# Chunk pairs: input halves added by accumulating DMAs, the second pair's parts kept in DRAM, out products held back for two phases

## The chip, the cores and the metric

One core of one Trainium2 chip runs the whole program. The metric is the device time of one execution in microseconds. Five engines work side by side, each through its own list of instructions in order, and they wait for one another through semaphores: TensorE (PE; its weight loads are shown apart as PEld), VectorE (DVE), ScalarE (ACT), GpSimd (POOL) and SyncE (SP, which here only issues DMAs). An instruction that waits holds up all that stand behind it on its engine.

## The reference

Attention with a learned position bias, then a gated feed-forward network on its result:

```python
scores = q @ k.T / sqrt(64) + bias        # 4 batches, 8 heads, 576 positions
x = (softmax(scores) @ v)                 # as 2304 tokens of 512
gate = 1 / (1 + exp(-(x @ w_gate)))       # 512 x 1536
out = (gate * (x @ w_val)) @ w_out        # 1536 x 512
```

All is float32. Only the feed-forward part, the last 475 us, is touched by the change.

## The kernel before, in words

The attention part writes its result to DRAM as two halves, `xs` (1024 rows by 2304 tokens, to be added in pairs of 64 rows), and the reciprocals of the softmax sums, `rs`. An input piece for the feed-forward part is made by loading both halves (`load_x`, L796), adding them, and multiplying by the reciprocals (`load_r`, L805). The tokens are cut into six chunks of 384. Each float32 factor of a product is split into a high part, written by ScalarE with rounding to the matmul's format, and a low part, the difference, written by VectorE; a product is three matmuls: high x high, high x low, low x high.

*The first pass* (`run`, the loop over `order`) takes chunks 0 (A) and 1 (B) through the 12 blocks of 128 hidden units, in the order that `ORDER` writes out: 24 steps. A step has the gate products (`gates`, L887, 24 matmuls of 384 columns into the banks `pg` and `pu`), the out products of the step before (`outs`, `out`, L908, 9 matmuls of 512 columns into `po0` to `po2`, which is three groups of three), and the gating (`gated`, L895 to L898: sigmoid, product with a VectorE instruction, high part, low part). Beside it `convert` turns weight blocks into their parts: integer steps on VectorE (L190, L193, L196, L199), the high part on ScalarE (L850) and the low part on VectorE (L855). 30 of the 36 blocks are converted in this way, two in an A step and one in a B step. The converted gate weights are stored to DRAM (`scratch`, L859) for later.

In the same pass the inputs of chunks 2 and 3 are prepared. `pair_x` is a generator, and `XPIECES` says how many of its pieces run after which step: eight pieces that load two 192 KB halves each, add them on GpSimd (L931), load the reciprocals and multiply on VectorE (L944); four sums or differences of the quarters on GpSimd (L950: S1 to S4); and seven splits (ScalarE L958, VectorE L959).

*The phases* (`phase`) then take two chunks and two blocks at a time by a seven-product scheme (Strassen's, in Winograd's form): seven products of sums of inputs with sums of weights in place of eight. `STEPS` lists them. There are 24 phases, v = 0 to 11 for chunks 2 and 3 and v = 12 to 23 for chunks 4 and 5; an even v makes the gate's products, an odd v the value's. A phase step has 6 matmuls of 384 columns (L1054) into `pu` and `pg` by turns and, in six of seven steps, one group of three out products from the list `groups`. VectorE makes the additions and the gating (L1020), ScalarE empties the first bank (L1060) and makes sigmoids and high parts (L1028, L1038), GpSimd makes the low parts of the gated values (L1040).

The weights of phase v come from `unit(v, ...)`: "l" loads the stored blocks from `scratch` (L975, tile `um`), "t" makes four sums on GpSimd (L983, tile `ut`), "a" to "d" split them (ScalarE L995, VectorE L998). What a phase does beside its products is the list `beside[i]` for step i: "l" for v+2 at step 6, "t" for v+1 at step 0, "a" to "d" at steps 1 to 4, stores at steps 1, 3 and 5.

The inputs of chunks 4 and 5 (the second pair) go through `pair_x` in phases 1 to 10 too, in the tiles `xeven` and `xodd`, which chunks 0 and 1 have left; but their splits need the buffers of the first pair's parts, which come free only in phase 11, so `XPARTS` puts them into phases 11 and 12.

`take` hands out 4 KB buffers (per partition) from the pools `wfirst`, `wa` and `wb`, `give` returns them. Temporaries `st` share a pool of five (`wm`) with the converted weights. `store` (L921, L922) copies a finished `po` bank by ScalarE into a tile `ob`, of a pool of two, and sends it out.

The instructions of one engine run in the order in which these loops issue them. SP issues all DMAs of this part; GpSimd issues none.

Of the kernel before, what the change touches and what calls it, by code (L numbers as in the profile page):

```python
# [10 lines left out]
F32 = mybir.dt.float32  # L11
# [5 lines left out]
ALU = mybir.AluOpType  # L17
# [118 lines left out]
def tile_kernel(ctx, tc, q, k, v, small, w_gate, w_val, w_out, steps, lpos, xtab, lx, out, phases="0AB"):  # L136
# [4 lines left out]
    scratch = dram.tile([3 * DFF // 128, 128, 4, 128], F32, name="scratch")  # L141

    moe = Moe(tc, w_gate, w_val, w_out, scratch, xs, rs, out)
# [551 lines left out]
class Moe:  # L695
# [4 lines left out]
    def __init__(self, tc, w_gate, w_val, w_out, scratch, xs, rs, out):  # L700
        self.tc, self.nc, self.xs, self.rs, self.out_ = tc, tc.nc, xs, rs, out
# [213 lines left out]
    def store(self, c, t):  # L915
        n = 3 * c + t
        if c >= self.NC - 2 and n % 2:
            ob = self.pools["xin"].tile([128, 2, self.T], F32, name="xin").rearrange("p s t -> p (s t)")[:, 0:DM]
        else:
            ob = self.pools["ob"].tile([128, DM], F32, name="ob")  # L920
        self.nc.scalar.activation(out=ob, in_=self.po[c][t], func=AF.Copy)  # L921
        self.nc.sync.dma_start(out=self.out_[128 * n:128 * n + 128, :], in_=ob)  # L922

    def pair_x(self, c0, room):

        nc, x, loads, rows, parts = self.nc, {}, [], [], {}
        todo = [(c, kc) for c in (c0, c0 + 1) for kc in range(4)]
        name = lambda c, kc: f"A{c - c0 + 1}{kc // 2 + 1}"

        def add(j):  # L930
            nc.gpsimd.tensor_tensor(out=loads[j][:, 0], in0=loads[j][:, 0], in1=loads[j][:, 1], op=ALU.add)  # L931

        for j in range(len(todo) + 2):
            if j < len(todo):
                loads.append(self.load_x(*todo[j]))
            if 0 < j <= len(todo):
                add(j - 1)
                rows.append(self.load_r(*todo[j - 1]))
            if j > 1:
                c, kc = todo[j - 2]  # L940
                n = name(c, kc)
                if n not in x:
                    x[n] = room(n)
                nc.vector.tensor_tensor(  # L944
                    out=x[n][:, kc % 2], in0=loads[j - 2][:, 0], in1=rows[j - 2], op=ALU.mult)
            yield
        for o, a, b, op in (("S1", "A21", "A22", ALU.add), ("S3", "A11", "A21", ALU.subtract),
                            ("S2", "S1", "A11", ALU.subtract), ("S4", "A12", "S2", ALU.subtract)):
            x[o] = room(o)
            nc.gpsimd.tensor_tensor(out=x[o], in0=x[a], in1=x[b], op=op)  # L950
            if o == "S3":
                self.spare(x["A21"])
            yield
        self.parts[c0] = parts
        for n in ("A11", "S2", "A12", "S1", "S3", "S4", "A22"):
            hi = self.take([128, 2, self.T], F32R, "xh", "wa", "wb")
            lo = self.take([128, 2, self.T], F32R, "xl", "wa", "wb")
            nc.scalar.activation(out=hi, in_=x[n], func=AF.Copy)  # L958
            nc.vector.tensor_tensor(out=lo, in0=x[n], in1=hi.bitcast(F32), op=ALU.subtract)  # L959
            self.spare(x[n])  # L960
            parts[n] = hi, lo
            yield
# [121 lines left out]
    def run(self):  # L1084
# [4 lines left out]
        with ExitStack() as ph, tc.manual_schedule():  # L1089
            self.open(ph, "left", wa=SLOTS["wa"], wb=SLOTS["wb"], wm=WM, ob=2, sg=4, gv=6)  # L1090
# [4 lines left out]
            before, groups, stores, lows = None, [], [], []  # L1095
            xs = self.pair_x(2, lambda n: self.take([128, 2, self.T], F32, "xp", "wa", "wb"))
            for i, cf in enumerate(order):
# [13 lines left out]
                stored = before and before[1] == NF - 1  # L1111
# [3 lines left out]
                if stored:  # L1115
                    stores += [(0, t) for t in range(3)]
                if stores:
                    self.store(*stores.pop(0))
# [11 lines left out]
            for _ in xs:  # L1130
                pass

            def group(c, f, t, gh, gl):
                def do():
                    self.out(c, f, t, gh, gl)
                    if f == NF - 1:
                        stores.append((c, t))
                return do
# [3 lines left out]
            late, xs = [], iter(())  # L1142
            for v in range(NV):
# [3 lines left out]
                if v == 1:  # L1147
                    tiles = [self.pools[p].tile([128, 4, self.T], F32, name=n) for p in ("xeven", "xodd") for n in ("xhi", "xlo")]
                    homes = dict(zip(("A11", "A12", "A21", "A22", "S1", "S2", "S3", "S4"), (
                        y[:, 2 * e:2 * e + 2] for y in tiles for e in range(2))))  # L1150
                    xs, pieces = self.pair_x(4, homes.get), 14
# [57 lines left out]
```

## Time and profile before

| | us |
|---|---|
| median of three runs | 849.97 |
| the three runs | 843.79, 849.97, 853.77 |
| the profiled execution | 848.56 |
| its span | 846.5 |
| granted TensorE clock over the span | 0.978 |

The busy shares over the span are TensorE 94%, VectorE 77%, ScalarE 58%, GpSimd 50%. The profile shows one execution. Its span begins with the first instruction; times in the trace are counted from there. The attention part lasts to about 361, the first pass from there to 540, the phases to 833.5, and then twelve groups of out products are left. In the profile L12 is line 12 of the kernel, and `a<-b,c` means that tile a is written from tiles b and c. The chain of waits is followed back from the last instruction, at each step to what released it.

### The profile page before, as it was taken

To read this page: it belongs to the slowest core of one execution; us is meant where nothing else is said; L and a number is where in the kernel's file an instruction comes from. 1 tells how busy PE (TensorE), PEld (TensorE's weight loads), DVE (VectorE), ACT (ScalarE), POOL (GpSimd) and SP (SyncE) were. 2 spreads that over 40 slices of the span, in tenths; PEclk is the share of its full clock that TensorE was granted. 3 is DMA by queue.
4 is the path that set the end of the run, shared out by engine and by line. 5 is a ranking of instruction groups with operands and counts; after the bars stand their busy time and mean duration, and the time that the engine had idled before them with its cause. 6 is when DMAs were issued, how large, how long until landed. Compare 5 with 4: busy or idle time off the path is not lost.

```text
span 846.5 us, 17373 instructions
## 1 busy us (share of the span) xinstructions
PE 791.8 (94%) x6356; PEld 730.9 (86%) x6356; DVE 655.0 (77%) x1299; ACT 488.4 (58%) x1032; POOL 423.6 (50%) x476
## 2 busy tenths in 40 slices
PE   7999989999999988889997898978999999999997
PEld 4888879999999988878996797977889988899996
DVE  6788889999989988967887986457776787566673
ACT  5888588998989978834432343433334354334332
POOL 1333579999999979600021401154674353445430
PEclk9999999999999999989999898989999999999999
DMA  5532336565664687486669302145111102122001
GB/s 188 165 117 97 86 87 171 137 179 143 168 174 132 181 201 208 144 273 228 189 188 246 123 26 86 51 137 162 63 50 51 51 26 94 55 75 75 26 1 74
DMA packets 60931, 104.27 MB, mean 123 GB/s; under 512 B 6704, under 2 KB 28336, under 8 KB 60848
## 3 DMA queue, kind: packets, MB, share of 16 engines
q1 hardware_dynamic: 58544, 99.70, 40.2%
q10 hardware_dynamic: 2304, 3.47, 1.2%
q8 instruction: 50, 0.82, 0.4%
q14 instruction: 33, 0.27, 0.1%
HBM read 72.67 MB, written 21.05 MB: 111 GB/s over the span
## 4 chain that ended last, share of the span: by engine, by line
PE 61%; DVE 18%; DMA 7%; ACT 6%; issue 4%; POOL 2%; SPq 1%; DVEq 0%; ACTq 0%; POOLq 0%
PE po L908 12%; PE sc L549 7%; PE pu L1054 7%; PE pg L1054 7%; PE acc L629 7%; PE pt L572 5%; PE pu L887 4%; PE pg L887 4%; PE bps L342 3%; DMA xin<-xs 2%; DVE st L1020 2%; PE y L318 2%; DVE sg L1020 2%; ACT ind L323 2%; DMA um<-scratch 2%
## 5 line engine op out<-in xcount | busy, mean ns | idle before, releaser
L908 PE MATMUL po<-w,gh 128*128 128x512 f32 x432 | 136.2, 396 | 0.0
L556 ACT ACTIVATE en<-en,mn 128x576 f32<-128x576 f32 x144 | 111.5, 775 | 30.4 <-DVE mn L553 29.2
L549 PE MATMUL sc<-k,QS 128*128 128x288 f32 x640 | 112.1, 301 | 3.1 <-POOL k L476 0.7
L553 DVE CUSTOM_DVE_ANT_0 en<-sc,bias 128x576 f32<-128x576 f32 x128 | 93.9, 753 | 7.5 <-PE sc L549 6.4
L983 POOL TENSOR_TENSOR ut<-um 128x256 f32<-128x256 f32 x48 | 40.7, 868 | 110.6 <-DMA um<-scratch 55.5
L549 PEld LDWEIGHTS sc<-k,QS 128*128 128x128 f32 x640 | 91.7, 188 | 5.0 <-POOL k L476 1.2
L572 PE MATMUL pt<-ident,en 128*128 128x128 f32 x576 | 86.9, 273 | 3.4 <-DVE aL L472 2.3
L908 PE MATMUL po<-w,gl 128*128 128x512 f32 x216 | 85.5, 396 | 0.6 <-DVE gl L1040 0.6
L629 PE MATMUL acc<-aH,vv 128*128 128x288 f32 x256 | 80.3, 331 | 5.2 <-DVE xe L632 5.1
L1040 POOL TENSOR_TENSOR gl<-sg,gh 128x384 fp32r<-128x384 f32 x44 | 49.2, 1118 | 70.4 <-ACT gh L1038 48.0
L908 PEld LDWEIGHTS po<-w,gh 128*128 128x128 f32 x432 | 80.0, 190 | 4.8
L1038 ACT ACTIVATE gh<-sg 128x384 fp32r<-128x384 f32 x48 | 25.2, 525 | 93.9 <-DVE sg L1020 93.8
L572 PEld LDWEIGHTS pt<-ident,en 128*128 128x128 f32 x576 | 68.9, 141 | 6.2 <-ACT en L556 2.9
L472 DVE TENSOR_TENSOR aL<-pt,aH 128x512 fp32r<-128x512 f32 (+1 forms) x112 | 66.7, 608 | 7.2 <-ACT aH L471 7.2
L629 PE MATMUL acc<-aL,vv 128*128 128x288 f32 x256 | 71.0, 295 | 0.0
L342 PE MATMUL bps<-cfs,ind 128*128 128x64 bf16 x1458 | 67.4, 193 | 3.2 <-DVE bias L358 2.2
L323 ACT ACTIVATE ind<-y 128x576 bf16<-128x576 f32 x100 | 62.4, 657 | 11.0 <-PE y L318 8.9
L931 POOL TENSOR_TENSOR xin<-xin 128x384 f32<-128x384 f32 x16 | 18.3, 1155 | 97.9 <-DMA xin<-xs 79.1
L342 PEld LDWEIGHTS <-ind 128*128 128x128 bf16 x1458 | 58.6, 98 | 9.9 <-DVE bias L358 4.1
L887 PE MATMUL pu<-xhi,w 128*128 128x384 f32 x192 | 58.0, 363 | 9.4 <-DVE sg L896 9.0
L476 POOL TENSOR_TENSOR aL<-ar,aH 128x512 fp32r<-128x512 f32 x48 | 62.8, 1308 | 4.0
L1028 ACT ACTIVATE sg<-sg 128x384 f32<-128x384 f32 x48 | 25.2, 525 | 65.8 <-DVE sg L1020 65.8
(171 smaller groups left out, 2245.9 us busy)
## 6 DMA issues: line engine op xcount, KB each, us to landing
um<-scratch SPq DMA_DIRECT2D x48, 256.0 KB, 2.7
kr<-in_k_dram SPq DMA_DIRECT2D x32, 288.0 KB
QS<-part SPq DMA_DIRECT2D x64, 144.0 KB, 2.8
xs<-xe SPq DMA_DIRECT2D x32, 288.0 KB, 3.6
xin<-xs SPq DMA_DIRECT2D x48, 192.0 KB, 3.3
vr<-in_v_dram SPq DMA_DIRECT2D x16, 320.0 KB, 3.8
scratch<-wm SPq DMA_DIRECT2D x20, 256.0 KB, 2.2
qr<-in_q_dram SPq DMA_DIRECT2D x16, 288.0 KB
```

The lines of the kernel that those rows point to most:

```text
L323: nc.scalar.activation(out=o, in_=y[:, :, 0:HF], func=AF.Sigmoid, scale=float(2.0 ** 64))
L342: nc.tensor.matmul(out=o, lhsT=st, rhs=cfs[:, part], start=(part == 0), stop=(part == 2))
L472: return lambda: nc.vector.tensor_tensor(out=lo, in0=ps, in1=hi.bitcast(F32), op=ALU.subtract)
L476: nc.gpsimd.tensor_tensor(out=lo, in0=src, in1=hi.bitcast(F32), op=ALU.subtract)
L549: nc.tensor.matmul(out=ps[:, e, 0:HF], lhsT=l, rhs=r[:, HF * e:HF * e + HF], start=(i == 0), stop=(i == len(mms) - 1))
L553: nc.vector.tensor_tensor_reduce(out=half(en), in0=ps[:, :, 0:HF], in1=half(nbias), scale=-0.125, scalar=3.0e38, op0=ALU.add, op1=ALU.min, ...
L556: nc.scalar.activation(out=en, in_=en, func=AF.Exp, bias=mn, scale=-1.0, accum_out=sm)
L572: nc.tensor.transpose(pt[:, J], en[:, 128 * J:128 * J + 128], ident)
L629: nc.tensor.matmul(out=acc[:, 0:HF], lhsT=l, rhs=r, start=(i == 0), stop=(i == len(mms) - 1))
L887: self.nc.tensor.matmul(out=(pg, pu)[z], lhsT=l, rhs=r, start=(kc == 0 and i == 0), stop=(kc == 3 and i == 2))
L908: self.nc.tensor.matmul(out=self.po[c][t], lhsT=l[:, tt], rhs=r, start=(f == 0 and i == 0), stop=(f == self.NF - 1 and i == 2))
L1054: nc.tensor.matmul(out=y, lhsT=l, rhs=r, start=(n == 0), stop=(n == 5))
```

## The change

- `pair_x` becomes a function that runs named steps, listed for the first pass in `XPIECES` and for the phases in `XSTEPS`. "L" loads the first halves (SP), "A" adds the second halves onto them by DMAs with `accum_op=ALU.add` that GpSimd issues, "r" loads reciprocals, "M" multiplies on VectorE. Each step of these moves 64 rows of 384 at a time (96 KB), and two pieces share an `xin` tile.
- The sums S1 to S4 are made by VectorE; S3 is written over A21.
- "P" splits as before (first pair). For the second pair "Q" splits in phases 8 to 10: the high part into one tile `high`, the low part in place, and both are written to DRAM (`xparts`). "R" loads them in phase 11 into the buffers that the first pair's parts leave.
- The out products of steps 20 to 22 of the first pass are not issued in the pass but appended to `groups` (`HELD`), as those of step 23 were before, so twelve groups go into phases 0 and 1, and the stores of chunk 0 with them.
- "l" of unit v+2 is issued at step 2 of a phase, not at step 6.
- The tiles `ob` come from the pool of five (`wm`); `wb` has 17 buffers, not 16. "l0" to "d" of the first unit stand one step later in `UPIECES`.

```diff
-SLOTS = {"wfirst": 6, "wa": 15, "wb": 16}
-XPIECES = {8: 2, 9: 1, 10: 2, 11: 1, 12: 2, 13: 1, 14: 2, 15: 1, 16: 2, 17: 1, 18: 2, 19: 1, 20: 2, 21: 2, 22: 2, 23: 9}
-XPARTS = {11: (1, 3, 4, 6), 12: (0, 2, 4)}
-UPIECES = {18: "l0", 19: "t0", 20: "l1", 21: "a0 b0", 22: "c0 d0"}
+SLOTS = {"wfirst": 6, "wa": 15, "wb": 17}
+HELD = 20
+XPIECES = {
+    6: "L0 L1", 8: "A0 A1 r0 r1", 9: "L2 L3", 10: "M0", 11: "M1 r2 r3 A2 A3", 12: "L4 L5", 13: "M2", 14: "M3 r4 r5 A4 A5",
+    15: "L6 L7", 16: "M4", 17: "M5 r6 r7 A6 A7", 18: "M6", 19: "M7", 20: "S1 S3", 21: "S2 S4", 22: "PA11 PS2 PA12",
+    23: "PS1 PS3 PS4 PA22"}
+UPIECES = {19: "l0", 20: "t0 l1", 21: "a0 b0", 22: "c0", 23: "d0"}
+XSTEPS = {
+    (0, 1): "L0 L1 r0 r1", (0, 3): "L2 L3", (1, 1): "A0 A1", (1, 4): "A2 A3", (2, 0): "M0", (2, 1): "M1 r2 r3", (2, 2): "L4 L5",
+    (2, 4): "M2", (2, 5): "M3 r4 r5", (3, 1): "A4 A5", (3, 2): "L6 L7", (4, 0): "M4", (4, 1): "M5 r6 r7", (4, 2): "A6 A7",
+    (4, 5): "M6", (4, 6): "M7", (6, 0): "S1", (6, 2): "S3", (6, 4): "S2", (7, 0): "S4", (8, 0): "QA22", (8, 2): "QA12",
+    (8, 4): "QS1", (9, 0): "QS3", (10, 0): "QS4", (10, 2): "QA11", (10, 4): "QS2", (11, 0): "RA11", (11, 1): "RS2",
+    (11, 2): "RA12", (11, 3): "RS1", (11, 4): "RS3", (11, 5): "RS4", (11, 6): "RA22"}
...
+    xparts = dram.tile([7, 2, 128, 2, 384], F32, name="xparts")
...
-            ob = self.pools["ob"].tile([128, DM], F32, name="ob")
+            ob = self.pools["wm"].tile([128, DM], F32, tag="wm", name="ob")
...
+            if k in "LA":
...
+                for e in range(2):
+                    row = 256 * kc + 128 * e + (64 if k == "A" else 0)
+                    src = self.xs[row:row + 64, T * c:T * c + T]
+                    if k == "L":
+                        nc.sync.dma_start(out=half(j)[64 * e:64 * e + 64], in_=src)
+                    else:
+                        nc.gpsimd.dma_start(out=half(j)[64 * e:64 * e + 64], in_=src, accum_op=ALU.add)
...
+                x[n] = x["A21"] if n == "S3" else room(n)
+                nc.vector.tensor_tensor(out=x[n], in0=x[a], in1=x[b], op=op)
...
+            elif k == "Q":
+                hi, i = room("high"), order.index(n)
+                nc.scalar.activation(out=hi.bitcast(F32R), in_=x[n], func=AF.Copy)
+                nc.vector.tensor_tensor(out=x[n].bitcast(F32R), in0=x[n], in1=hi, op=ALU.subtract)
+                for z, t in enumerate((hi, x[n])):
+                    nc.sync.dma_start(out=self.xparts[i, z], in_=t)
+            else:
+                parts[n] = [self.take([128, 2, T], F32R, "xr", "wa", "wb") for _ in range(2)]
+                for z, t in enumerate(parts[n]):
+                    nc.sync.dma_start(out=t.bitcast(F32), in_=self.xparts[order.index(n), z])
...
-                    self.outs(*before)
+                    if i <= HELD:
+                        self.outs(*before)
+                    else:
+                        groups += [group(before[0], before[1], t, *before[2:]) for t in range(3)]
...
-                for _ in range(XPIECES.get(i, 0)):
-                    next(xs, None)
+                xs(XPIECES.get(i, ""))
...
+                for i in range(7):
+                    if (v, i) in XSTEPS:
+                        beside[i].append(lambda w=XSTEPS[v, i]: xs(w))
                 if v + 2 < NV:
-                    beside[6].append(lambda v=v: self.unit(v + 2, "l"))
+                    beside[2].append(lambda v=v: self.unit(v + 2, "l"))
```

## Rows read from the trace of the kernel before

**Rows 1.** Stages: us, busy PE, PEld, DVE, ACT, POOL, clock, DMA share, GB/s.
```profile
372.00:424.20 52.20, 51.40 (x256) 48.18 (x257) 41.77 (x79) 22.48 (x43) 0.00 (x0) 0.94 0.71 234
424.20:517.50 93.30, 80.34 (x388) 73.94 (x387) 80.58 (x127) 33.72 (x63) 19.06 (x14) 0.91 0.49 141
540.40:563.60 23.20, 18.47 (x94) 16.98 (x94) 12.40 (x24) 9.45 (x19) 5.69 (x6) 0.91 0.41 126
563.60:675.40 111.80, 107.44 (x541) 96.51 (x540) 81.11 (x126) 40.24 (x82) 65.21 (x67) 0.99 0.25 74
675.40:703.80 28.40, 25.43 (x122) 22.75 (x122) 22.38 (x33) 14.28 (x27) 12.10 (x12) 0.94 0.13 44
```

**Rows 2.** Chain of waits, first pass: start us, us, what.
```profile
420.00 2.08 PE pg L887 x12
...
424.16 2.05 PE po L908 x9
...
477.48 2.23 DVE wm L196
...
516.64 3.02 PE pu L887 x12
...
540.38 1.04 PE pu L1054 x6
```

**Rows 3.** VectorE's groups, 393 to 424.2: instruction, shapes, count | busy us, mean ns | idle before.
```profile
L199 DVE SCALAR_TENSOR_TENSOR wm<-ww,wm 128x512 int32<-128x512 int32 x8 | 5.5, 692 | 0.3
L855 DVE TENSOR_TENSOR w<-wm,w 128x512 fp32r<-128x512 f32 x8 | 5.5, 685 | 0.0
L190 DVE TENSOR_SCALAR wm<-wm 128x512 f32<-128x512 f32 x9 | 3.8, 420 | 0.0
L193 DVE TENSOR_SCALAR wm<-wm 128x512 int32<-128x512 int32 x8 | 3.4, 420 | 0.0
```

**Rows 4.** VectorE's groups, 424.2 to 517.5.
```profile
L199 DVE SCALAR_TENSOR_TENSOR wm<-ww,wm 128x512 int32<-128x512 int32 x18 | 15.5, 860 | 0.6
L855 DVE TENSOR_TENSOR w<-wm,w 128x512 fp32r<-128x512 f32 x20 | 15.0, 752 | 0.0
L196 DVE SCALAR_TENSOR_TENSOR wm<-ww,wm 128x512 int32<-128x512 int32 x18 | 14.0, 776 | 0.6
L193 DVE TENSOR_SCALAR wm<-wm 128x512 int32<-128x512 int32 x18 | 10.0, 557 | 0.0
L190 DVE TENSOR_SCALAR wm<-wm 128x512 f32<-128x512 f32 x17 | 9.5, 561 | 0.0
L898 DVE TENSOR_TENSOR gl<-sg,gh 128x384 fp32r<-128x384 f32 x12 | 6.7, 559 | 7.1 <-ACT gh L897 7.1
...
L944 DVE TENSOR_TENSOR xp<-xin,xrec 128x384 f32<-128x384 f32 x8 | 5.3, 659 | 3.0 <-DMA xrec<-rs 3.0
L959 DVE TENSOR_TENSOR xl<-xp,xh 128x768 fp32r<-128x768 f32 x4 | 3.8, 953 | 1.0 <-ACT xh L958 1.0
```

**Rows 5.** GpSimd's groups, 424.2 to 517.5.
```profile
L931 POOL TENSOR_TENSOR xin<-xin 128x384 f32<-128x384 f32 x8 | 8.8, 1103 | 94.5 <-DMA xin<-xs 79.1 <-DVE wm L190 8.4 <-DVE wm L196 7.0
L950 POOL TENSOR_TENSOR xp<-xp 128x768 f32<-128x768 f32 x4 | 8.5, 2141 | 10.9 <-DVE xp L944 10.8
```

**Rows 6.** Chain of waits, phase 1.
```profile
551.79 4.50 DMA um<-scratch
```

**Rows 7.** Chain of waits, a phase at full pace.
```profile
763.02 1.04 PE pg L1054 x6
764.06 1.06 PE pu L1054 x6
765.11 0.70 PE po L908 x3
```

**Rows 8.** Line L796: issues on SP's queue, ns least/median/most, first and last start.
```profile
L796 SPq DMA_DIRECT2D xin<-xs x48: 573/605/946, 292.6 to 595.5; - x48
```

**Rows 9.** DMA issues by line: count, KB each, median us from issue to landing.
```profile
xin<-xs SPq DMA_DIRECT2D x48, 192.0 KB, 3.3
```

More of the change, by code (lines that the diff above doesn't have):

```diff
@@ L698, with __init__ @@
     NC = NT // T
[L700 to L701 removed]
+    def __init__(self, tc, w_gate, w_val, w_out, scratch, xparts, xs, rs, out):
+        self.tc, self.nc, self.xs, self.rs, self.out_, self.xparts = tc, tc.nc, xs, rs, out, xparts
         self.src = {}
@@ L927, in pair_x @@
[L927 to L941, printed above, removed]
+        nc, T = self.nc, self.T
@@ new lines, in pair_x, with do, half, one @@
+        x, loads, rows = {}, {}, {}
+        parts = self.parts[c0] = {}
+        order = [a for a, _ in self.STEPS]
+        def do(what):
+            for w in what.split():
+                one(w[0], w[1:])
+        def half(j):
+            return loads[j // 2][:, j % 2]
+        def one(k, n):
+            j = int(n) if k in "LArM" else 0
+            c, kc = c0 + j // 4, j % 4
+            if k in "LA":
+                if k == "L" and j % 2 == 0:
+                    loads[j // 2] = self.pools["xin"].tile([128, 2, T], F32, name="xin")
+                for e in range(2):
[5 more added lines that the diff above has]
+                        nc.gpsimd.dma_start(out=half(j)[64 * e:64 * e + 64], in_=src, accum_op=ALU.add)
+            elif k == "r":
+                rows[j] = self.load_r(c, kc)
+            elif k == "M":
+                n = f"A{c - c0 + 1}{kc // 2 + 1}"
@@ L942, in pair_x @@
                 if n not in x:
                     x[n] = room(n)
[L944 to L962, printed above, removed]
+                nc.vector.tensor_tensor(out=x[n][:, kc % 2], in0=half(j), in1=rows[j], op=ALU.mult)
+            elif k == "S":
+                n = k + n
+                a, b, op = self.SUMS[n]
+                x[n] = x["A21"] if n == "S3" else room(n)
+                nc.vector.tensor_tensor(out=x[n], in0=x[a], in1=x[b], op=op)
+            elif k == "P":
+                hi = self.take([128, 2, T], F32R, "xh", "wa", "wb")
+                lo = self.take([128, 2, T], F32R, "xl", "wa", "wb")
+                nc.scalar.activation(out=hi, in_=x[n], func=AF.Copy)
+                nc.vector.tensor_tensor(out=lo, in0=x[n], in1=hi.bitcast(F32), op=ALU.subtract)
+                self.spare(x[n])
+                parts[n] = hi, lo
+            elif k == "Q":
[8 more added lines that the diff above has]
+                    nc.sync.dma_start(out=t.bitcast(F32), in_=self.xparts[order.index(n), z])
@@ L1129, in run @@
                 g()
[L1130 to L1138, printed above, removed]
             groups += [group(before[0], before[1], t, *before[2:]) for t in range(3)]
             NV = 2 * NF
-            late, xs = [], iter(())
+            tiles = [self.pools[p].tile([128, 4, self.T], F32, name=n) for p in ("xeven", "xodd") for n in ("xhi", "xlo")]
+            homes = dict(zip(("A11", "A12", "A21", "A22", "S1", "S2", "S4", "high"), (
+                y[:, 2 * e:2 * e + 2] for y in tiles for e in range(2))))
+            late, xs = [], self.pair_x(4, homes.get)
             for v in range(NV):
```

31 lines of the change are left out of this document (11 added, 20 removed).

## The prediction

> **What bounds the kernel now.** I read the table of stages first. The reader is to see that TensorE is the nominal limit, busy for all but a few us of most stages, and that three stages are exceptions: 424.2 to 517.5 (80.3 us busy of 93.3, granted clock 0.91), 540.4 to 563.6 (18.5 of 23.2, clock 0.91) and 675.4 to 703.8 (25.4 of 28.4, clock 0.94) [rows 1]. Only there can time be won, unless matmuls go, and none do.
>
> Second, the chain in order of time through the first pass. At full pace a step is 2.08 us for each of the two gate products and 2.05 for the out products, 6.21 us in all. Step 8 begins at 420.00 and the first phase at 540.38: 120.4 us for 16 steps that need 99.4, so 21.0 are lost [rows 2]. The chain there goes through VectorE: VectorE paces this stretch, and TensorE waits for converted weights or for a bank to be emptied.
>
> Third, VectorE's groups, before the pair loads begin and while they run. A conversion is five instructions, 0.69 (L199, and L196, which is the same operation on the same shape), 0.69, 0.42 and 0.42 us at pace [rows 3]. In the loaded stretch the same five mean 0.86, 0.78, 0.75, 0.56 and 0.56 [rows 4]. In that stretch GpSimd makes eight adds of 1.10 us and four sums of 2.14 us [rows 5], and beside a sum VectorE's 0.69 us instruction takes 2.23 [rows 2]. So GpSimd's arithmetic costs VectorE its own time. Besides, VectorE stands 3.0 us in its multiply for reciprocals that have not landed, and 1.0 us for ScalarE in the splits [rows 4].
>
> **The change, first pass.** What VectorE is relieved of up to the end of the conversions, from [rows 3, 4]: (860-692)x18 = 3.0, (752-685)x20 = 1.3, (776-692)x18 = 1.5, (557-420)x18 = 2.5, (561-420)x17 = 2.4, together 10.7; the multiplies lose 0.8 more (659 against 559 for the other 384-wide instruction, x8). The waits of 3.0 and 1.0 go, since each half is now loaded two steps before its accumulate and the accumulate about two before the multiply, some 12 us each, where a load lands in 3.3 [rows 9]. Four split subtractions of 0.95 (3.8 us) move behind the conversions. Sum: 19.3 us.
>
> That assumes that an accumulating DMA does not hold VectorE back. The trace of before has no DMA issued by GpSimd. At worst each holds VectorE as the add did, the adds' share of 11.5 us: 11.5 x 8.8/17.3 = 5.9. At best nothing is held; a gain below nothing is not to be had, as the lock of the adds is counted already. I take nothing, since no elements of the input pass through GpSimd any more, and keep 5.9 for the range.
>
> The gate products of step 20 end at 519.66 now [rows 2]. Less 19.3 that is 500.4. TensorE alone would be there at 420.00 + 12x6.21 + 4.16 = 498.7, so VectorE is still last, by 1.7.
>
> From there to the first phase it is 20.7 us now. In the changed kernel TensorE has 2.05 (out products of step 19) and three steps of 4.16, 14.5, because nine held groups (9x0.70) leave. VectorE has more than before: the four sums, at 0.95 each by the 768-wide subtraction of [rows 4], and the splits. I walk it: gating (0.56, a wait of 7.1/12 = 0.59 for ScalarE, 0.56, [rows 4]) and two sums end at 504.0; the gate products of step 21 are there at 506.6; gating, two sums and a unit's low part (0.69, as the same 512-wide instruction of [rows 3]) end at 510.9; step 22 is there, gating, three splits (3x0.95+1.0) and a low part end at 517.2; the multiply of step 23 frees the bank at 517.7. So the first phase starts at **517.7** instead of 540.4. If VectorE hid behind TensorE it would be 514.9; if nothing is won in these steps, 521.1. The four remaining splits (3.8 us) then delay phase 0's own additions, and a phase step with its groups lasts 1.75: I put 1.5 us for it.
>
> **The phases.** At pace a step is 1.05 and a group 0.70 [rows 7]; 24 phases have 168 steps. Now 135 groups lie between the start and 833.5, so 270.9 of 293.1 us: 22.2 lost. In the changed kernel 144 groups lie there (the held twelve fill phases 0 and 1 with six each): 277.2 us, then the tail after 833.5, 13.0, unchanged. The losses by stage [rows 1], before and then after:
> - Phases 0 and 1: 23.2 less 14x1.05+3x0.70 is 6.4. The chain shows a weight load that is on its way only from 551.8, for 4.5 us, then GpSimd's differences [rows 6]. The load now stands at step 2 of a phase, not step 6, behind eight input loads of 0.6 [rows 8] and one store: about 7 us into phase 0, where it is at 11 now, and the phase is 2.1 longer. Next late are the four splits: 1.5.
> - Phases 2 to 10: 111.8 less 9x11.55 is 7.9. GpSimd's adds and sums go; four sums (3.8) and seven split subtractions (6.7) come to VectorE, which is busy 81 of 112 us there: room for them. Added waits: ScalarE may not write the single `high` tile again before its 384 KB write to DRAM has landed. A 192 KB load lands in 3.3 [rows 9], and writes follow by two steps, 3.5: between nothing and 1 us, three times. SP now waits for each split before it issues; behind it stand weight loads with some 8 us in hand. I take 3.5.
> - Phases 11 and 12: 28.4 less 23.1 is 5.3, the splits of the second pair. They become 14 loads, 5.5 MB. The DMA rate at full share is 141/0.49 to 234/0.71, 288 to 330 GB/s [rows 1]: 2.4 to 2.7 us for a pair of loads, one pair issued every 1.65, each due some 10 after. With one weight load between, the seventh lands about 23 after phase 11's start and is due at 21.5. At 330 it costs nothing, at the unscaled 234 some 7. I take 2.5, near the rate at full share.
> - Phases 13 to 23: the rest of the 22.2, 2.6; a weight load issued at step 6 can be late there too, and step 2 gives it 7 us more; 1.0.
>
> Sum: 517.7 + 277.2 + 1.5+3.5+2.5+1.0 + 13.0 = 816.4 us of span against 846.5. The profiled execution took 848.56, 2.06 over its span, and stands 1.4 below the median shown: 816.4+2.06+1.4 = **820**. The extra buffer slot and the out buffers taken from the shared pool cost nothing where they are hidden by TensorE; if a store held the pool, a temporary waits for a landing of some 2 us, in phases 0, 1, 12 and 13 only.
>
> **What GpSimd's queue does.** It loses 16 adds and 8 sums, 35 us at [rows 5]'s means, and gets 32 DMA issues. Bounds of one: nothing, or as long as a load takes to be issued and to land, 0.95+3.3 = 4.2 [rows 8, 9], if the engine were held; I take 1.0, nearest to SP's 0.6 and to the add it replaces. In phases 2 to 10 GpSimd is busy 65.2 us; less eight adds and four sums (17.4) that is 5.3 a phase. In phases 1 to 4 (46.2 us) it has 21.2 to do and 16 issues: full only at 1.6 us each. In the first pass it has nothing else.
>
> The Trainium skill speaks against this part ("DMA: Bandwidth & Descriptors", SWDGE vs HWDGE vs iDMA): for a DMA issued from GpSimd the descriptors are written by GpSimd into SBUF, state that VectorE shuts it out of in its two-port mode, and a DMA issued from SP is immune. By that rule the issues would be slowest where VectorE is fullest. No run here shows it yet; the rival below prices it.
>
> **Rivals.**
> 1. *Slower: GpSimd's queue paces phases 1 to 4.* The weight differences stand behind the accumulates in order. Decides from 1.6 us per issue; at 4.2 it is 16x4.2+21.2 = 88.4 in 46.2, 42 late: 862. For it: nothing like it was measured, VectorE is dense. Against: SP issues in 0.6.
> 2. *No change: the accumulated halves land late, or wait for the first half, so VectorE stands at the multiplies as it does now.* Eight multiplies that each wait the 3.0 us which [rows 4] has for all of them give back 24: 844. Against it: about 24 us of lead.
> 3. *Half the gain: VectorE stays locked by the accumulates (5.9) and the parts come late from DRAM (5 more than taken):* 831.
> 4. *Better: VectorE hides behind TensorE and the phase losses nearly vanish:* 514.9+277.2+2+13.0+3.5 = 811, or below.
>
> **How the numbers follow.** Forecast 820 (811 to 829): 0.60. Rival 3: 0.13. Rival 2: 0.10. Rival 1: 0.12. Below 811: 0.05. The range 809 to 845 leaves out rival 1 and the far ends of the others. One per cent, 8.5 us, is about what a measurement of this kernel can tell from no change. Faster by more: forecast, rival 3, the low end and nothing of rival 2: 0.77. Within: 0.11. Slower: 0.12.
>
> **What would show it.** Right: first phase near 518; VectorE's 0.42 us instructions at 0.42 between 424 and 500; no wait of VectorE for a load at the multiply; weight differences in phase 1 ready before the step that needs them; no split in phases 11 and 12, and TensorE waiting there at most 3 us, for loads. Wrong: GpSimd holding over 1.6 us per accumulate, or VectorE waiting at multiplies; TensorE waiting for parts from DRAM through phase 12; VectorE so full in steps 20 to 23 that the first phase starts after 521.

## The result and the profile after

The changed kernel takes 821.25 us (median of four runs, 819.7 to 825.87); the kernel before took 847.29 in the four runs that count beside it. A fifth run of the changed kernel, 817.06, is not in that median. The ratio is 0.9682, with a 95% interval from 0.961 to 0.9753: faster, by 26 us, where 820 was forecast in a range of 809 to 845.

The profiled execution is the slowest of these runs, 825.87 us with a span of 824.1. Its attention part is 2.1 us longer than before (step 8 of the first pass begins at 421.96, not at 419.83), which the change doesn't touch. So I compare stages by their length, each from its first matmul to that of the next, read from the timeline of TensorE:

| stage | before | forecast | after |
|---|---|---|---|
| first pass, step 8 to phase 0 | 120.4 | 97.7 | 101.1 |
| phases 0 and 1 (nine groups more after) | 23.4 | 24.6 | 27.8 |
| phases 2 to 10 | 111.8 | 107.5 | 109.3 |
| phases 11 and 12 | 28.4 | 25.6 | 23.2 |
| phases 13 to 23 | 129.7 | 128.1 | 127.4 |
| the rest | 13.0 | 13.0 | 13.3 |

The stages of the changed kernel, with the columns of [rows 1]; the first is the 93.4 us from step 8's out products on, the others are the stages of the table:

```profile
426.30:519.70 93.40, 89.67 (x477) 84.00 (x476) 76.10 (x136) 36.24 (x68) 13.76 (x16) 1.00 0.52 151
523.10:550.90 27.80, 25.13 (x121) 22.74 (x122) 19.30 (x30) 13.95 (x26) 15.21 (x18) 0.95 0.41 110
550.90:660.20 109.30, 105.72 (x542) 95.85 (x540) 89.10 (x137) 45.69 (x91) 61.20 (x65) 1.00 0.39 122
660.20:683.40 23.20, 23.20 (x121) 21.47 (x122) 17.00 (x27) 10.16 (x21) 10.71 (x13) 1.00 0.87 314
683.40:810.90 127.50, 127.50 (x662) 117.99 (x662) 87.94 (x142) 48.06 (x100) 53.70 (x59) 1.00 0.15 48
```

TensorE is busy for 89.7 of 93.4 us where it was for 80.3 of 93.3, and its granted clock there is 1.00 in place of 0.91. In phases 11 and 12 and from 13 on the profile shows no idle time of it.

The clock has a part of its own in this. In the kernel before, it was granted at 0.50, the lower of its two levels (1.2 GHz), in three stretches of together 17 us, from 463.9, 484.4 and 511.7 on, each time in or right after a wait of TensorE of 3.7 to 4.4 us; the last of them, in the columns of [rows 1]:

```profile
511.70:518.50 6.80, 5.43 (x17) 5.43 (x18) 5.49 (x8) 2.50 (x5) 2.67 (x3) 0.50 0.11 42
```

The gate product of 3.02 us in [rows 2], which takes 2.08 at pace, lies for the most part in it. In the changed kernel the clock does not fall from step 8 until the wait just ahead of phase 0.

VectorE's groups over the same 93.4 us answer to [rows 4] (all line numbers from here on are ten to forty higher than before):

```profile
L865 DVE TENSOR_TENSOR w<-wm,w 128x512 fp32r<-128x512 f32 x20 | 14.1, 711 | 0.0
L206 DVE SCALAR_TENSOR_TENSOR wm<-ww,wm 128x512 int32<-128x512 int32 x18 | 12.9, 715 | 0.6
L209 DVE SCALAR_TENSOR_TENSOR wm<-ww,wm 128x512 int32<-128x512 int32 x18 | 12.5, 692 | 0.6
...
L203 DVE TENSOR_SCALAR wm<-wm 128x512 int32<-128x512 int32 x18 | 8.3, 461 | 0.0
L200 DVE TENSOR_SCALAR wm<-wm 128x512 f32<-128x512 f32 x17 | 7.1, 419 | 0.0
L976 DVE TENSOR_TENSOR xp<-xin,xrec 128x384 f32<-128x384 f32 x8 | 4.4, 551 | 0.0
L981 DVE TENSOR_TENSOR xp<-xp 128x768 f32<-128x768 f32 x4 | 3.8, 955 | 0.1
```

A conversion is nearly back at its pace, and the multiplies (L976) wait for nothing. What took the place of GpSimd's adds: all 32 accumulating DMAs, the length of their records on GpSimd in ns (least, median, most), from the view of their line; one group of four of them from the timeline; and the stretches of this and of another group, in the columns of [rows 1]:

```profile
L969 POOL DMA_DIRECT2D xin<-xs x32: 803/1378/2185, 415.4 to 583.3; - x32
```
```profile
540.96 3.31 POOL L969 DMA_DIRECT2D xin<-xs  x4
```
```profile
540.96:544.27 3.31, 3.31 (x19) 3.08 (x18) 0.74 (x2) 0.65 (x2) 3.31 (x5) 1.00 0.82 216
546.84:550.19 3.35, 3.35 (x19) 3.08 (x19) 3.20 (x6) 1.31 (x3) 3.35 (x6) 1.00 0.52 112
```

The records of four issues in a row overlap, so their lengths do not add up: seven of the eight groups of four hold GpSimd for 3.3 to 3.5 us and the first, at 415.4, for 4.0. That is 0.8 to 1.0 us for each. The DMA issues with KB and median us to landing:

```profile
xr<-xparts SPq DMA_DIRECT2D x14, 384.0 KB, 4.8
xparts<-xlo SPq DMA_DIRECT2D x10, 384.0 KB, 2.3
...
xin<-xs POOLq DMA_DIRECT2D x32, 96.0 KB, 4.9
```

And the place that went worse than forecast, the splits on either side of the start of phase 0 (523.05); those shown stand before it, and the four behind it run in the same way. The timeline of VectorE, then that of ScalarE:

```profile
517.23 0.96 DVE L986 TENSOR_TENSOR xl<-xp,xh 128x768 fp32r<-128x768 f32 x1 [0.18 <-ACT xh L985]
519.10 0.96 DVE L986 TENSOR_TENSOR xl<-xp,xh 128x768 fp32r<-128x768 f32 x1 [0.91 <-ACT xh L985]
520.97 0.96 DVE L986 TENSOR_TENSOR xl<-xp,xh 128x768 fp32r<-128x768 f32 x1 [0.91 <-ACT xh L985]
```
```profile
516.37 0.83 ACT L985 ACTIVATE xh<-xp 128x768 fp32r<-128x768 f32 x1
518.23 0.85 ACT L985 ACTIVATE xh<-xp 128x768 fp32r<-128x768 f32 x1 [1.03 <-DVE xl L986]
520.10 0.84 ACT L985 ACTIVATE xh<-xp 128x768 fp32r<-128x768 f32 x1 [1.02 <-DVE xl L986]
```

The reader is to see a ring: VectorE's low part waits 0.91 us for ScalarE's high part, and the next high part waits 1.03 us for that low part. A split takes 1.87 us, not 0.95.

### The profile page after: what moved, and what is told of

It reads as the page before. It is cut to its first block, busy times and chain, and to the rows that moved or that the text cites. A ratio compares the mean times of both kernels' runs of the same rounds, so it can differ in the third digit from the quotient of the medians.

```text
span 824.1 us, 17460 instructions
## 1 busy us (share of the span) xinstructions
PE 780.7 (95%) x6356; PEld 724.8 (88%) x6356; DVE 656.4 (80%) x1307; ACT 487.8 (59%) x1032; POOL 419.1 (51%) x484
## 5 line engine op out<-in xcount | busy, mean ns | idle before, releaser
L1021 POOL TENSOR_TENSOR ut<-um 128x256 f32<-128x256 f32 x48 | 44.8, 955 | 77.3 <-DVE xl L986 30.5
L969 POOL DMA_DIRECT2D xin<-xs x32 | 27.5, 1328 | 103.0 <-DMA xin<-xs 65.4
L897 PE MATMUL pg<-xhi,w 128*128 128x384 f32 x192 | 55.1, 346 | 5.7 <-ACT sg L905 3.7
```

The source lines that it names most:

```text
L897: self.nc.tensor.matmul(out=(pg, pu)[z], lhsT=l, rhs=r, start=(kc == 0 and i == 0), stop=(kc == 3 and i == 2))
```

## The experiments

Eleven kernels were run, each beside the kernel before on the same chip. Their ratios have intervals of 0.2 to 0.5 per cent to either side, so that differences of 2 or 3 us between them are read from stage lengths of the profiles, not from the medians. Where the code of a stage is the same, the profiles differ too: phases 0 and 1 take 27.8 us in the changed kernel, at a granted clock of 0.95, and 28.7 and 28.8, at 0.88, in two kernels that differ from it elsewhere ("Nothing in DRAM" and "Loads shortly before their use"), and phases 2 to 10 take 109.3 and 110.4 in it and in the second of these. So one stage's difference of 1 us says nothing there; the pass, with 101.1, 101.1 and 101.3 us in three kernels with the same pass, is read more finely. Each expectation sets its theory A, the author's own reading at that time, against another.

**The groups issued in the pass again.**

```diff
-HELD = 20
+HELD = 23
```

> Undoes one part: the out products of steps 20 to 22 are issued in the pass again, only those of step 23 are held. Theory A (the gain of the first pass is VectorE's: locks and waits that went; the held groups only follow it): TensorE's three steps grow from 4.16 to 6.21 us, but VectorE paces them in the changed kernel (phase 0 begins 523.1, 4.5 after TensorE could), so phase 0 begins only 2 to 4 us later, and phases 0 and 1 have 6.2 us less to do; the whole within 3 us of the changed kernel's 821, at 818 to 824. Theory B (the held groups carry the gain by filling phases 0 and 1 while the weights come): 6 us or more slower, 827 and up.

Measured: 823.09 us, ratio 0.9737 (0.9706 to 0.9769). In this kernel chunk 0's three stores of 18 are missing, since the products that are issued in the pass don't queue them. The pass from step 8 on is 103.6 us (101.1 in the changed kernel), phases 0 and 1 are 25.6 (27.8), phases 2 to 10 are 110.5 (109.3). Together 1.5 us more. So A: holding the groups is worth little; they move work out of a place where VectorE was late anyway. As this kernel has three stores less to make, the 1.5 us are rather too few.

**The weight load at step 6 again.**

```diff
-                    beside[2].append(lambda v=v: self.unit(v + 2, "l"))
+                    beside[6].append(lambda v=v: self.unit(v + 2, "l"))
```

> Undoes one part: the weight load of unit v+2 stands at step 6 of a phase again. Theory A: the load for phase 2 is issued some 7 us later, lands late for the sums in phase 1, and phases 0 to 2 lose 3 to 6 us as before (6.4 there); later phases lose 1 to 2 more where a store or an input load stands before it: 825 to 829. Theory B (the held groups lengthen phases 0 and 1 so much that the load is in time at step 6 too): no difference, 819 to 823.

Measured: 838.34 us, ratio 0.9916 (0.9885 to 0.9947), 17 us slower than the changed kernel, far over what either theory said. The pass is unchanged (101.1), phases 2 to 10 take 119.3 (109.3), phases 11 and 12 take 26.6 (23.2), the rest of the phases 130.1 (127.4). Who waits, in the view of GpSimd's waits from phase 0 on, us in total, times, longest; of this kernel, to 680:

```profile
POOL ut L1021 <- DMA um<-scratch: 52.0, 7, 11.6
```

and of the changed kernel, to 690:

```profile
POOL ut L1021 <- DMA um<-scratch: 16.2, 4, 5.9
```

A wait of GpSimd is no loss by itself. But the chain of waits of this kernel goes through the load and the sums of weights behind it (L1021), and the load there stands on SP's queue behind a store of out products (L932):

```profile
548.23 0.34 SPq L932
548.68 0.37 SPq L1013
...
549.10 6.13 DMA um<-scratch
...
555.39 1.90 POOL ut L1021 x2
```

Between 530 and 720 the chain goes through such a load six times. Phases 2 and 3 lose the most, 3.6 and 4.5 us against the changed kernel, and phase 12 loses 3.3.

**The weight load at step 2 in the kernel before, alone.** The same line of the kernel before, `beside[6]` to `beside[2]`, nothing else.

> The kernel before with one part of the change alone: the weight load of unit v+2 at step 2 of a phase in place of step 6. Theory A (the load was late in the kernel before too, and this is a part of the gain by itself): phases 0 and 1 get back about 5 of the 6.4 us that they lost, phases 3 to 5 some 3 and phase 15 about 1.6: 835 to 840 against 846. Theory B (the early load is needed only because the changed kernel puts input loads and part writes on the same queue, which is what the 17 us of undoing it in the changed kernel show): 843 to 846.

Measured: 841.17 us, ratio 0.9921 (0.9895 to 0.9947), some 6 us faster than before. Phases 0 and 1 are 19.3 us (23.4), phases 2 to 10 are 109.9 (111.8), the rest within 0.6 of before. The time lies between the ranges of A and B, nearer to A, and phases 0 and 1 get back 4.1 us of A's 5. So the load was late in the kernel before as well, and moving it is a part of the gain by itself; but undoing it costs 17 and doing it alone brings 6. A reason for the difference is what the change itself puts on the queues: 28 transfers of parts on SP's, 16 accumulates on GpSimd's list, behind which the sums of weights stand, and the stores of chunk 0 in the first phases. That is argued: no run takes these off one by one.

**The sums on GpSimd again.**

```diff
-                nc.vector.tensor_tensor(out=x[n], in0=x[a], in1=x[b], op=op)
+                nc.gpsimd.tensor_tensor(out=x[n], in0=x[a], in1=x[b], op=op)
```

> Undoes one part: the four sums of each pair are made by GpSimd again, in the same places. Theory A (GpSimd's arithmetic holds VectorE back): a sum takes 2.1 us on GpSimd and stops VectorE for about as long; VectorE is spared 3.8 us but the sums stand in a row right before the splits, 8.6 us, where VectorE paces: phase 0 begins 3 to 6 us later, and the second pair's phases lose 0 to 2: 824 to 829. Theory B (the sums cost nothing wherever they are, the gain was that loads came earlier): 819 to 823.

Measured: 820.83 us, ratio 0.9706 (0.9673 to 0.9739): no difference. The pass is even 1.4 us shorter (99.7); phases 0 and 1 are 1.0 longer (28.8) and phases 2 to 10 are 0.7 longer, no more than profiles differ there. The sums run at 2 us each, as before the change, but in steps 20 and 21, where VectorE waits for TensorE up to 2.6 us at a time in the changed kernel:

```profile
494.24 4.38 POOL L981 TENSOR_TENSOR xp<-xp 128x768 f32<-128x768 f32 x2 [21.15 <-DVE xp L976]
...
501.92 3.78 POOL L981 TENSOR_TENSOR xp<-xp 128x768 f32<-128x768 f32 x2
```

The sums still hold VectorE back: two low parts of conversions take 2.93 us together in place of 1.29, and two of the gating 1.05 and 1.93 in place of 0.56 each. But between them VectorE waits 4.0 us for TensorE, and it no longer has to make the sums, which were 3.8 us. In the kernel before, the four sums stood beside a conversion, and four instructions that take 0.42 to 0.69 us at pace took 2.0 to 2.2 each, 6.3 us more in all; two of them, and the sums:

```profile
475.37 2.08 DVE L193 TENSOR_SCALAR wm<-wm 128x512 int32<-128x512 int32 x1
477.48 2.22 DVE L196 SCALAR_TENSOR_TENSOR wm<-ww,wm 128x512 int32<-128x512 int32 x1
```
```profile
475.02 8.57 POOL L950 TENSOR_TENSOR xp<-xp 128x768 f32<-128x768 f32 x4 [10.79 <-DVE xp L944]
```

A falls here in one point: what counts is where the sums stand, not on which engine. The 1.4 us that the pass wins come from elsewhere: with the sums ahead of it on GpSimd's list, the first weight differences come at 498.6, behind the last conversions and not beside them, and TensorE loses 2.5 us in step 20 in place of 4.0.

**Nothing in DRAM.** Q and R are taken out of `XSTEPS`; the second pair is split in place in phases 11 and 12:

```diff
-    (4, 5): "M6", (4, 6): "M7", (6, 0): "S1", (6, 2): "S3", (6, 4): "S2", (7, 0): "S4", (8, 0): "QA22", (8, 2): "QA12",
...
+    (4, 5): "M6", (4, 6): "M7", (6, 0): "S1", (6, 2): "S3", (6, 4): "S2", (7, 0): "S4", (11, 1): "PA11", (11, 3): "PS2", (11, 4): "PA12", (11, 6): "PS1",
+    (12, 0): "PS3", (12, 2): "PS4", (12, 4): "PA22"}
```

> Undoes one part: nothing goes to DRAM; the second pair is split in phases 11 and 12 as before the change. Theory A: phases 11 and 12 lose some 5 us again (5.3 before, 0.1 in the changed kernel), while phases 8 to 10 get back the 3.6 us that they lose in the changed kernel, so the parts in DRAM are worth 1 to 3 us: 821 to 825. Theory B (the DRAM parts are worth all of the 5 us, the losses of phases 8 to 10 have another cause): 825 to 828.

Measured: 823.83 us, ratio 0.9734 (0.9701 to 0.9767). Phases 11 and 12, in the columns of [rows 1]:

```profile
651.40:680.30 28.90, 24.35 (x121) 21.16 (x120) 22.75 (x33) 14.24 (x27) 13.13 (x14) 1.00 0.15 46
```

28.9 us against 23.2 with the parts in DRAM, 5.7 more; phases 2 to 10 take 105.6 against 109.3, 3.7 less. A: the parts in DRAM save the whole loss of phases 11 and 12 and give most of it back in phases 8 and 10 (13.5 us each, 11.7 without them); 2 us remain.

**GpSimd arithmetic put back, with nobody waiting for it.**

```diff
                 nc.vector.tensor_tensor(out=x[n][:, kc % 2], in0=half(j), in1=rows[j], op=ALU.mult)
+                nc.gpsimd.tensor_tensor(out=half(j), in0=half(j), in1=rows[j], op=ALU.mult)
```

> The changed kernel with 16 GpSimd multiplies more, one after each multiply of an input piece (128x384, into the piece's own buffer after its last use, which no output reads): as much GpSimd arithmetic as the 16 adds that the change removed, but nobody waits for its result. Theory A (GpSimd's arithmetic holds VectorE back where VectorE paces): the eight in the first pass take some 5 us from VectorE, the conversions end that much later, and the whole is 3 to 6 us slower: 824 to 827. Theory C (VectorE has room there now; what was won in the pass was the waits for loads, and the lock only where VectorE had none to spare): 820 to 822.

Measured: 837.14 us, ratio 0.9891 (0.9867 to 0.9915), 16 us slower. The pass is 5.0 us longer (106.1). Phases 2 to 10 are 11.7 us longer, which neither theory had:

```profile
551.80:672.80 121.00, 108.91 (x542) 96.86 (x541) 92.73 (x137) 46.00 (x91) 70.81 (x73) 0.99 0.36 110
```

In the pass five of the eight multiplies stand beside a conversion and hold one of its instructions back by 0.8 us each, 4.1 us in all: four times the 0.42 us instruction of L203 takes 1.22 to 1.25, and once two low parts take 2.10 in place of 1.29. The other three fall on times at which VectorE waits for ScalarE, and cost it nothing. So in the pass it is A, at 4.1 of its 5 us. The first of the five, and the row of that instruction:

```profile
438.71 1.39 POOL L977 TENSOR_TENSOR xin<-xin,xrec 128x384 f32<-128x384 f32 x1 [25.05 <-DVE xp L976]
```
```profile
439.14 1.24 DVE L203 TENSOR_SCALAR wm<-wm 128x512 int32<-128x512 int32 x1
```
```profile
L203 DVE TENSOR_SCALAR wm<-wm 128x512 int32<-128x512 int32 x18 | 10.8, 602 | 0.0
```

Against the changed kernel this row is (602-461)x18 = 2.5 us longer, as the first weight differences, which hold three conversion instructions back there, come only at 501.8 here, beside the last one. The rest of the 5.0 is not separated; in it are a wait of VectorE of 1.4 us at a multiply, whose accumulates were issued 70.2 us after the start of step 8 in place of 54.4, and a granted clock of 0.96 over the stretch in place of 1.00.

The 11.7 are at least partly order. The multiply on GpSimd waits for VectorE's and holds the accumulates and the sums of weights behind it, and VectorE then waits for an accumulate, 5.4 us at one time. Phases 2 and 3 are 1.8 and 3.1 us longer, phase 5, with that wait, 6.0. The chain of waits there goes through GpSimd's list:

```profile
590.26 1.54 POOL xin L969 x2
591.79 6.28 DMA xin<-xs
...
598.21 1.38 PE pu L1093 x6
```

How much of the 11.7 is time taken from VectorE was not separated.

**The splits' buffers given back one later.**

```diff
-                self.spare(x[n])
+                if parts:
+                    self.spare(x[list(parts)[-1]])
                 parts[n] = hi, lo
+                if len(parts) == 7:
+                    self.spare(x[n])
```

> The changed kernel with the first pair's splits freed later: a split returns its source buffer only after the next split has taken its two, so that ScalarE's next high part need not wait for VectorE's low part. Theory A (the buffer just returned is taken at once, which makes a split 1.87 us in a row of them instead of 0.95, and this is why the first phase began 3 us later than forecast and phase 0 lost 4.7): phase 0 begins 2 to 3 us earlier and loses some 3 less: 815 to 818. Theory B (the splits are bound by something else, the two engines' exchange): 820 to 822.

Measured: 818.60 us, ratio 0.9667 (0.9641 to 0.9694). The ring is gone; VectorE's low parts follow one another:

```profile
514.41 2.83 DVE L986 TENSOR_TENSOR xl<-xp,xh 128x768 fp32r<-128x768 f32 x3 [0.18 <-ACT xh L985]
519.63 3.70 DVE L986 TENSOR_TENSOR xl<-xp,xh 128x768 fp32r<-128x768 f32 x4 [0.18 <-ACT xh L985]
```

ScalarE's waits for VectorE's low parts, us in total, times, longest, in the changed kernel and in this one:

```profile
ACT xh L985 <- DVE xl L986: 5.1, 5, 1.0
```
```profile
ACT xh L985 <- DVE xl L986: 0.6, 2, 0.3
```

The pass is 1.6 us shorter (99.5), phases 0 and 1 are 2.3 shorter (25.5). A, a little less than it said. The cause is shown, since the order in which buffers are returned is all that was changed: `take` gives the next high part a buffer of the first pool with one free, which was the one that the last source had just left, and ScalarE had to wait until VectorE had read that source. Not all of the 2.3 us are waits: the granted clock over phases 0 and 1 is 1.00 here and 0.95 in the changed kernel, and TensorE's busy time for the same work is 23.8 us in place of 25.1.

**The same, with step 20's products in the pass** (`HELD = 21`, and chunk 0's stores queued there).

> As the run before it, and the products of step 20 are issued in the pass (chunk 0's stores are then queued as before). Theory A: VectorE still has more to do than TensorE in steps 21 to 23, so three groups there cost nothing, and phases 0 and 1 have 2.1 us less: 0 to 2 us faster than the run before it, 814 to 817. Theory B (with the splits faster TensorE paces steps 21 to 23): equal within 1 us.

Measured: 818.65 us, ratio 0.9667 (0.9643 to 0.9692): equal, as B said. The pass is 2.1 longer, phases 0 and 1 are 0.7 shorter; phases 2 to 10, which this edit does not touch, are 1.7 longer in its profile (111.1).

**Loads shortly before their use.**

```diff
-    6: "L0 L1", 8: "A0 A1 r0 r1", 9: "L2 L3", 10: "M0", 11: "M1 r2 r3 A2 A3", 12: "L4 L5", 13: "M2", 14: "M3 r4 r5 A4 A5",
-    15: "L6 L7", 16: "M4", 17: "M5 r6 r7 A6 A7", 18: "M6", 19: "M7", 20: "S1 S3", 21: "S2 S4", 22: "PA11 PS2 PA12",
+    9: "L0 L1 A0 A1 r0 r1", 10: "M0", 11: "M1", 12: "L2 L3 A2 A3 r2 r3", 13: "M2", 14: "M3", 15: "L4 L5 A4 A5 r4 r5",
+    16: "M4", 17: "M5 L6 L7 A6 A7 r6 r7", 18: "M6", 19: "M7", 20: "S1 S3", 21: "S2 S4", 22: "PA11 PS2 PA12",
```

> The changed kernel's first pass with the loads of a pair of pieces, their accumulates and their reciprocals all issued one step before the multiply (steps 9, 12, 15 and 17 in place of 6 to 17 with two steps between each); the multiplies stay where they are but for none. Theory A (the second half of the first pass's gain is that no multiply waits): a load lands in 3.7, an accumulate takes 1.4 to issue and 4.9 to land, together 10 us, against 6.2 of lead, so VectorE stands some 4 us at each of the four first multiplies, and as it has about 5 us to spare in steps 8 to 19, the first phase begins 8 to 12 us later: 829 to 833. Theory C (only GpSimd's arithmetic mattered, waits are absorbed): within 2 us of 821.

Measured: 824.84 us, ratio 0.9735 (0.9682 to 0.9788); the pass takes 101.4 us, 0.3 more than in the changed kernel, and no multiply waits. The run didn't test what it was made for: SP issues the loads of step 9 at 429.9, early in that step, and the multiply stands at the end of VectorE's list of step 10, so the lead was still some 12 us, enough for the 10 that load and accumulate take. So both theories stay open, and that the waits of [rows 4] went because of the earlier loads stays argued.

**Both losses mended.** As in the run with the buffers, and the second pair's low part made a step after its high part:

```diff
-                nc.vector.tensor_tensor(out=x[n].bitcast(F32R), in0=x[n], in1=hi, op=ALU.subtract)
-                for z, t in enumerate((hi, x[n])):
-                    nc.sync.dma_start(out=self.xparts[i, z], in_=t)
+                nc.sync.dma_start(out=self.xparts[i, 0], in_=hi)
+                x["hi"] = hi
+            elif k == "q":
+                nc.vector.tensor_tensor(out=x[n].bitcast(F32R), in0=x[n], in1=x["hi"], op=ALU.subtract)
+                nc.sync.dma_start(out=self.xparts[order.index(n), 1], in_=x[n])
```

with "qA22" at (8, 1), "qA12" at (8, 3), and so on, one step after each "Q".

> The changed kernel with the splits of the first pair freed one later (as in the run with that alone) and the second pair's splits in two: ScalarE's high part in a step and VectorE's low part one step later, so that VectorE does not stand behind ScalarE. Theory A (phases 8 and 10 lose 2 us each because VectorE, in order, waits 0.7 to 1.7 us for ScalarE at each low part): those losses go, 3 us less than the run with the first edit alone: 814 to 817. Theory B (the losses come from VectorE's load in those phases): 818 to 819.

Measured: 816.53 us, ratio 0.9656 (0.9619 to 0.9694), six runs. Phases 2 to 10 take 106.9 us (109.4 in the run with the buffers alone), but phases 11 and 12 take 24.5 (23.3): a part of the loss moved on. Phases 8 and 10 take 11.6 us each, in place of 13.5, so their losses were VectorE's waits for ScalarE (5.1 us in three waits and 1.8 in four, in the changed kernel's phases 2 to 10), as A said. But phases 9 and 11 now take 12.9 each, in place of 11.6: VectorE's low part itself (L999) stands there before the sum that TensorE waits for, and beside GpSimd's sums of weights it takes 1.50 us where 0.95 is its pace. In phase 9:

```profile
626.71 1.50 DVE xhi L999
628.21 0.48 DVE sg L1064
```

So 1.3 us of the 3.8 remain won, and the rest is VectorE's own load, as theory B had it.

**The same with the sums on GpSimd.**

> As the run before it, with the sums made by GpSimd. Theory A (in steps 20 and 21 VectorE stands waiting for TensorE in any case, and with the splits faster the sums are what is late): 1 to 3 us slower than the run before it. Theory B (as with the sums alone undone): equal within 1.5 us.

Measured: 815.33 us, ratio 0.9641 (0.9607 to 0.9676): B, equal within 1.5 us. The pass takes 97.7 us (99.3 in the run before), phases 0 and 1 take 25.5. So with the splits mended too, the sums on GpSimd make the pass shorter, by 1.6 us. Both kernels are below the changed one's 821.25, and from step 8 on their profiles are 397.0 and 396.2 us long, where the changed kernel's is 402.1; they are the best that was run.

## Why the prediction was right, point by point

*VectorE paces the first pass; relieved, it gives TensorE's time back.* Right. From step 8 to step 20 the changed kernel takes 74.6 us, 12 full steps of 6.21, where it took 89.0. The gate products of step 20 end 16.9 us earlier, counted from step 8, where the sum had 19.3; in the 16.9 is the clock, which no longer falls, and for which the sum has no term. The five conversion instructions gained 9.0 of the 10.7 us forecast ([rows 4] less the rows after: 0.8, 1.1, 3.0, 1.7, 2.4). The missing 1.7 has a cause in the rows: GpSimd's first weight differences ("t0", 496.7 to 500.4) now fall on the last conversions, whose instructions take 1.21, 0.95 and 1.11 us there in place of 0.69, 0.42 and 0.69:

```profile
496.69 1.72 POOL L1021 TENSOR_TENSOR ut<-um 128x256 f32<-128x256 f32 x2 [16.92 <-PE po L918]
```
```profile
497.75 1.21 DVE L865 TENSOR_TENSOR w<-wm,w 128x512 fp32r<-128x512 f32 x1
498.88 0.95 DVE L203 TENSOR_SCALAR wm<-wm 128x512 int32<-128x512 int32 x1
499.87 1.11 DVE L206 SCALAR_TENSOR_TENSOR wm<-ww,wm 128x512 int32<-128x512 int32 x1
```

The prediction said that GpSimd has nothing else to do in the first pass than the issues; it left t0 out. TensorE lost 4.0 us in step 20, where I had put 1.7, and 2.5 in the run with the sums on GpSimd, where t0 comes behind the conversions.

*An accumulating DMA does not hold VectorE back.* Right, within 0.2 us. In the four groups of issues from 415.4 to 479.8 the conversions run at pace but for two instructions, of 0.50 and 0.53 in place of 0.42; the first of them is in the 3.5 us of four issues from 460.25:

```profile
460.54 0.50 DVE L203 TENSOR_SCALAR wm<-wm 128x512 int32<-128x512 int32 x1
461.07 0.69 DVE L206 SCALAR_TENSOR_TENSOR wm<-ww,wm 128x512 int32<-128x512 int32 x1
461.80 0.69 DVE L209 SCALAR_TENSOR_TENSOR wm<-ww,wm 128x512 int32<-128x512 int32 x1
462.40 0.42 DVE L200 TENSOR_SCALAR wm<-wm 128x512 f32<-128x512 f32 x1
```

*GpSimd's adds cost VectorE time.* Shown by the run with eight multiplies put back, which took 4.1 us from VectorE's conversions, against the 5.9 that I had as the share of eight adds. The Trainium skill has the rule ("SBUF — State Buffer", SBUF: two separate sides): GpSimd and VectorE share a pair of ports that one holds for a whole instruction while the other stands. The 2.23 us of [rows 2] beside sums of 2.14 [rows 5] agree with it. For the sums the price was of their place: beside a conversion they cost 6.3 us in the kernel before, and the run with the sums on GpSimd lost nothing.

*The splits at 0.95 us.* The step that was mis-sized. I priced seven splits by the instruction alone and one wait of 1.0; they took 1.87 each, as the buffer of one had to be read before the next could begin. It made the pass about 1.6 us longer and phases 0 and 1 about 2.3, the clock's share included, as the run with the buffers shows, of 3.4 and 3.2 over the forecast. Phase 0 begins at 523.05, which is 520.9 without the 2.1 us of the attention part; the prediction had named a start after 521 as a sign against it.

*The weight load at step 2.* Right in direction and undervalued. I gave it some 5 us of phases 0 and 1 and a little after; alone it brings 6, and without it the changed kernel loses 17. What the sum lacked is that its terms hang together: the weight loads have "some 8 us in hand" behind the queues' new work only because they stand early.

*Held groups.* I took their 6.2 us out of steps 21 to 23 and put them into phases 0 and 1, at no gain; right: holding them is worth some 1.5 us.

*The parts in DRAM.* Phases 11 and 12 lose nothing, where I had 2.5: a load of 384 KB lands in 4.8 us, and all transfers of these phases together run at 314 GB/s, inside the 288 to 330 that I had scaled. Phases 2 to 10 lost 5.3 where I had 3.5. The share of ScalarE's wait was named (up to 1 us three times, for the `high` tile), but the profile shows no wait of ScalarE for that tile, and the wait that came is another: VectorE, in order, waits up to 1.7 us for the high part that ScalarE has still to make.

*GpSimd's queue.* Four issues hold it for 3.3 to 3.4 us in phases 1 to 4, so one costs some 0.84, against 1.0 taken and 1.6 from which it would decide; the 1.38 in the median are records that overlap. The slower rival was not near: 16x0.84 = 13.4 us of the 25 that GpSimd had free. Its mechanism is real, though: with 16 multiplies more on GpSimd's list the accumulates came late, and phases 2 to 10 took 11.7 us more. The Trainium skill's rule on descriptors ("DMA: Bandwidth & Descriptors", SWDGE vs HWDGE vs iDMA) that I had cited would, as the prediction read it, slow issues where VectorE is full. This trace hardly shows it, and it does not show which of VectorE's instructions run in the two-port mode that the rule speaks of: four issues take 3.31 us with VectorE busy for 0.74 of them and 3.35 with VectorE busy for 3.20, and once 4.0, beside VectorE busy for 3.9.

*The no-change rival* (multiplies that wait) didn't come: no wait in the pass. The chances that the prediction adds up for a faster kernel (0.60, 0.13, 0.05) make 0.78, not 0.77. Of the sum, the pass was 3.4 too short, phases 0 and 1 were 3.2 and phases 2 to 10 were 1.8 too short, phases 11 to 23 were 3.1 too long. In the profiled execution the span is 7.7 us over the 816.4 that I summed, 2.1 of it in the attention part; that execution is 4.6 us above the median of its kernel, where the one of before lies 1.3 above its own, so part of the nearness of 820 to 821.25 is luck. The part before step 8 is the same code everywhere, and yet step 8 begins between 414.9 and 422.0 in the profiles of the thirteen kernels; the stages behind it missed the sum by 5.6 us together, more than the median shows.

## What to carry to other kernels

When work is moved off one engine's list or queue, look at what the freed order lets come early, and at what the added transfers put behind them: here the weight load of each phase, issued four steps earlier, cost 17 us when it was undone, and brought a third of that when it was done alone. Price a repeated pair of instructions on two engines by its period, with the buffer that the second hands back, not by the instruction's length. And ask of work on an engine that holds another back beside what it lands: the same sums cost VectorE 6.3 us beside a conversion and nothing where it would have waited for TensorE anyway.

## What was not expected of the hardware

Four accumulating DMAs of 64 rows by 1536 bytes in a row hold GpSimd for 3.3 to 3.5 us, with VectorE busy for 0.7 to 3.2 of them (once for 4.0, beside a VectorE that was busy for 3.9), and one lands after 4.9 us in the median, while a plain one of the same size, issued by SP, lands after 3.7. With the 14 loads of 384 KB the DMAs moved 314 GB/s over 23 us, at a DMA share of 0.87, and slowed no other engine's work that the rows show: TensorE was busy throughout. And a wait of TensorE costs more than its own length where the clock falls with it: a gate product that takes 2.08 us at pace took 3.02, most of it at 1.2 GHz, behind a wait of 3.7.
